# Inverse roots in ten instructions, and transposes moved by one product, in the z2 stage of a gated MLP

## The chip, the cores and the metric

One core of a Trainium2 chip runs the whole program. The time is the device time of one execution in microseconds (us). Engines are named as in the profile: PE is the matmul engine (PEld its weight loads), DVE the vector engine, ACT the scalar engine, POOL the GpSimd engine, SP the engine that only issues DMAs here.

## The reference

A block with two branches over 2048 rows of 576 features. The first branch normalises the rows, convolves them with a long kernel (a state-space model) and adds the result to x. The second branch is a gated MLP, and the change lies at its beginning:

```
h = _layernorm(x) * (1 + cb) + sb               # 2048 x 576
z = gelu(h @ w_in)                              # 2048 x 4608
z1 = z[:, :2304];  z2 = _layernorm(z[:, 2304:])
g = w_sp @ z2 + b_sp[:, None]                   # 2048 x 2048 by 2048 x 2304
x = x + gb * ((z1 * g) @ w_out)
```

The layer norm is `(x - mean) / sqrt(var + 1e-5)` over a row.

## The kernel before

The program runs three stages one behind the other. The first branch takes some 435 us. Then comes the z2 stage (`phase_a`), which computes z2 for all rows and stores it. The last stage (`phase_b`) computes z1, g and the output in four quarters.

In the z2 stage the rows are 16 tiles of 128, b = 0 to 15. All engines run the instructions in the order in which the Python code writes them: `self.tied` pins every instruction of an engine behind the one written before it, so the order of the calls is the order of each engine's queue. The loop `for b in range(1, 16)` writes one iteration per tile:

- `ln2_stats(b+3)`, `roots`, `ln2_rows(b+2)` (DVE): statistics, inverse root and normalised rows `n2` of a coming tile. In the profile the rows are written by two SCALAR_TENSOR_TENSOR and a COPY on `n`.
- `turn(b+1)` (PE): five transposes of `n2` with `ident` into the PSUM tile `pt`, of which there is one.
- `turn_hi(b+1)` (ACT) copies `pt` as fp16 into `nt`; `turn_lo(b+1)` (DVE) writes the rest, `pt - nt`, into the other half of `nt` and stores `nt` in DRAM (`n2_d`) on POOL's queue. A value is thus held as two fp16 numbers, and a product takes 14 matmuls per 512 columns. The first four need only the high part of `nt`, the ninth is the first to need the low part.
- `z2_mm(b, h)` (PE): five products `pz`, h = 0 to 3 of 512 columns and h = 4 of 256. `pz` has six PSUM buffers.
- `z2_gelu(b, h)` (ACT): gelu of a product into the two halves `z2` of the tile (1152 columns each; the profile calls them `z`). The pool has four such halves, so a tile's first gelu waits until the first half of the tile two before it has been stored.
- `z2_stats(b, c)` (DVE): statistics of six pieces of 384 columns (`bsz`). `roots(b-1, b+2)` takes the inverse roots of z2's variance of tile b-1 and of the coming tile's rows in one go (`rsqrt`, two columns `128x2`).
- `z2_diff(b-1)` (DVE, for even b-1 only) subtracts the halves; `z2_norm(b-1)` (ACT) applies the affine map with the root to both halves, `z<-z,nm,r` in the profile; `z2_store(b-1)` (POOL queue) stores them in `z2_d`.
- `do(b, LD)` to `do(b, V1)` are side work: weights of later stages are loaded, squared for their norms, scaled and split. In iterations 9 to 15 the side work prepares the blocks `wsp` of `w_sp`: `block_load` (SP) reads one into the single tile `xz`, `wsp_sums` (V0, DVE: three TENSOR_TENSOR on `xz`), `wsp_hi` (A1, ACT), `wsp_lo` (V1, DVE), and the next `block_load` waits for that `wsp_lo`.

`rsqrt` is also called four times in the first branch (`128x4`), and behind the loop `roots(15)`, `z2_norm(15)` and `z2_store(15)` end the stage. PE then has four products of z1 to do (`ps<-n2q,wf`), and needs from DVE and ACT the sets `zset` for g's first products (`ps<-wsp,zset`); the work on these stands behind `roots(15)` on DVE.

Of the kernel before, what the change touches and what calls it, by code (L numbers as in the profile page):

```python
# [9 lines left out]
F32 = mybir.dt.float32  # L10
F16 = mybir.dt.float16
BF = mybir.dt.bfloat16
I32 = mybir.dt.int32
AF = mybir.ActivationFunctionType
ALU = mybir.AluOpType
# [7 lines left out]
FH = 2304  # L23
# [166 lines left out]
def ssm(tc, I, x1_d, consts_s, dram, mod_d, mlp):  # L190
# [5 lines left out]
    with ExitStack() as ctx:  # L196
# [246 lines left out]
        def ln_stat(i, b):  # L443
# [22 lines left out]
            if b < 4:  # L466
                bs, mv = lnt[i]
                for h in range(2):
                    V.bn_stats(bs[:, b, h], x[:, b, HC * h:HC * h + HC])
                V.bn_aggr(mv[:, b], bs[:, b])  # L470
            else:
                mv = lnt.pop(i)[1]
                nm = ep.tile([128, 4], F32, name="nm")
                r = ep.tile([128, 4], F32, name="r")
                V.tensor_scalar(nm, mv[:, :, 0], -1.0, None, op0=ALU.mult)
                rsqrt(V, ep, r, mv[:, :, 1], 4)
                lns[i] = nm, r
# [497 lines left out]
def rsqrt(V, pool, r, var, n):  # L975

    vh = pool.tile([128, n], F32, name="vh%d" % n)
    q = pool.tile([128, n], F32, name="rq%d" % n)
    V.tensor_scalar(vh, var, 1e-5, 0.5, op0=ALU.add, op1=ALU.mult)
    V.tensor_single_scalar(q.bitcast(I32), vh.bitcast(I32), 1, op=ALU.logical_shift_right)  # L980
    V.tensor_scalar(r.bitcast(I32), q.bitcast(I32), -1, 0x5F3759DF - 0x400000, op0=ALU.mult, op1=ALU.add)

    for i in range(3):
        V.tensor_tensor(q, r, r, op=ALU.mult)
        V.tensor_tensor(q, q, vh, op=ALU.mult)
        if i < 2:
            V.scalar_tensor_tensor(r, q, 1.5, r, op0=ALU.subtract, op1=ALU.mult)
    V.tensor_scalar(q, q, -1.0, 1.5, op0=ALU.mult, op1=ALU.add)
    V.tensor_tensor(r, r, q, op=ALU.mult)


class Mixed:
# [7 lines left out]
class Mlp:  # L1000
# [428 lines left out]
    def z2_gelu(self, b, h):  # L1429
        n = min(512, FH - 512 * h)  # L1430
        if h == 0:
            self.zs[b] = [self.zp.tile([128, FH // 2], F32, name="z2", bufs=4) for _ in range(2)]
            self.bz[b] = self.ap.tile([128, 6, 6], F32, name="bsz")
        pm, c0 = self.pzs.pop((b, h)), 512 * h
        for i, z in enumerate(self.zs[b]):
            a, e = max(c0, FH // 2 * i), min(c0 + n, FH // 2 * (i + 1))
            if a < e:
                self.nc.scalar.activation(z[:, a - FH // 2 * i:e - FH // 2 * i], pm[:, a - c0:e - c0], AF.Gelu_apprx_tanh,
                                          scale=self.wcol(5 + h, INV_IN))
# [27 lines left out]
    def phase_a(self):  # L1467
        self.n2o, self.n2t, self.wrs = {}, {}, {}
        self.prods, self.z1s, self.n2, self.bsp, self.gbs, self.wfs = {}, {}, {}, {}, {}, {}
        ap = self.ap = self.pool(self.c2, "ap", 2)  # L1470
        cpa = ExitStack()
        self.pa = self.pool(cpa, "pa", 6, space=PSUM)
        self.ps1 = lambda: self.pa.tile([128, 512], F32, name="pz")
        self.zp = self.pool(self.c2, "zp", 2)
        self.wp = self.pool(self.ctx, "wp", 7, side="right")

        self.bq = self.pool(self.ctx, "bq", 1, side="right")
        self.cfp = self.ctx.enter_context(ExitStack())
        self.fp = self.pool(self.cfp, "fp", 1, side="right")
        self.wso = ap.tile([128, 4, 10, 128], F16, name="wso", bufs=1)  # L1480
        self.nc, plain = self.tied, self.nc
        self.nc.vector.memset(self.wso[64:, :, 9], 0.0)

        LD, PE, A0, A1, V0, V1 = range(6)
        sides = [[[] for _ in range(6)] for _ in range(17)]

        def side(b, k, fn, *a):
            sides[b][k].append((fn, a))

        def do(b, k):  # L1490
            for fn, a in sides[b][k]:
                fn(*a)

        for q in range(5):
            side(2 * q, LD, self.side_load, q)
            side(2 * q + 1, A0, self.side_sum, q)
            side(2 * q + 1, PE, self.win_scale, q)
            side(2 * q + 1, A1, self.side_hi, q)
            side(2 * q + 1, V1, self.side_last, q)
            side(2 * q + 1, V1, self.side_lo, q, 0)  # L1500
            side(2 * q + 2, V0, self.side_lo, q, 1)
        for h in range(2):
            side(1, LD, self.bsp_load, ap, h)
            side(2, A0, self.norm_bsp, h)
        for i in range(8):
            side(2 + i // 2, A1, self.wsp_load, 0, i, ap)
            side(3 + i // 2, A0, self.norm_sp, 0, i)
        for i in range(12):
            side(6 + i // 2, A1, self.out_load, ap, i)
            side(7 + i // 2, A0, self.norm_out, i)  # L1510
        for i in range(6):
            side(12 + i // 2, A1, self.wsp_load, 1, i, ap)
            side(13 + i // 2, A0, self.norm_sp, 1, i)
        side(13, V1, self.sums_out)
        side(14, PE, self.scales_out)
        side(6, V1, self.sums_sp, 0)
        side(7, PE, self.scales_sp, 0)
        side(11, PE, self.scales_gate, 0)
        side(12, PE, self.scale_p, 0)
        for i in range(7):  # L1520
            side(9 + i, V0, self.wsp_sums, i)
            side(9 + i, A1, self.wsp_hi, 0, i)
            side(9 + i, V1, self.wsp_lo, 0, i)
            side(8 + i, V1, self.block_load, 0, i)
        side(12, LD, self.z1_rows, 0)
        side(14, LD, self.bias_load, 0)
        for f, b in ((0, 14), (9, 15), (1, 15)):
            side(b, LD, self.z1_load, 0, f)


        self.turn(0)
        self.turn_hi(0)
        self.start_lo(2)
        self.start_load(4)
        self.x1_load(4)
        self.turn_lo(0)
        roots12 = self.ln2_two(1)
        do(0, LD)
        self.z2_mm(0, 0)
        do(0, A0)  # L1540
        self.start_sum(3)
        self.win_scale(8)
        self.z2_gelu(0, 0)
        self.start_hi(3)
        roots12()
        self.ln2_rows(1)
        do(0, PE)
        self.z2_mm(0, 1)
        self.z2_gelu(0, 1)
        self.start_sum(4)  # L1550
        self.z2_mm(0, 2)
        self.turn(1)
        self.start_lo(3)
        self.win_scale(9)
        self.turn_hi(1)
        self.start_hi(4)
        self.turn_lo(1)
        do(0, V0)
        self.z2_gelu(0, 2)
        self.z2_mm(0, 3)  # L1560
        do(0, A1)
        self.start_lo(4)
        self.ln2_rows(2)
        self.z2_stats(0, 0, 1, 2, 3)
        self.z2_gelu(0, 3)
        self.ln2_stats(3)
        do(0, V1)
        self.z2_stats(0, 4)
        self.z2_mm(0, 4)
        self.z2_gelu(0, 4)  # L1570
        for b in range(1, 16):
            do(b, LD)
            self.z2_mm(b, 0)
            do(b, A0)
            self.z2_gelu(b, 0)
            self.z2_stats(b - 1, 5)
            self.roots(b - 1, b + 2 if b + 2 < 16 else None)
            if b % 2:
                self.z2_diff(b - 1)
            self.z2_norm(b - 1)  # L1580
            if b + 2 < 16:
                self.ln2_rows(b + 2)
            if b + 4 < 16:
                self.x1_load(b + 4)
            self.z2_mm(b, 1)
            if b + 1 < 16:
                self.turn(b + 1)
            do(b, PE)
            self.z2_gelu(b, 1)
            self.z2_store(b - 1)  # L1590
            do(b, V0)
            self.z2_stats(b, 0, 1)
            if b + 1 < 16:
                self.turn_hi(b + 1)
            if b + 1 < 16:
                self.turn_lo(b + 1)
            self.z2_mm(b, 2)
            self.z2_gelu(b, 2)
            do(b, A1)
            self.z2_mm(b, 3)  # L1600
            self.z2_stats(b, 2, 3)
            self.z2_gelu(b, 3)
            if b + 3 < 16:
                self.ln2_stats(b + 3)
            do(b, V1)
            self.z2_stats(b, 4)
            self.z2_mm(b, 4)
            self.z2_gelu(b, 4)
        cpa.close()
        self.z2_stats(15, 5)  # L1610
        self.roots(15)
        self.z2_norm(15)
        self.z2_store(15)
        self.nc = plain
        self.c2.close()
# [652 lines left out]
S_H, I_H, S_O, I_O, N_S, N_O, N_H, N_B, _, T0, T1, HB, N_P = range(13)  # L2268
# [64 lines left out]
```

## Time and profile before

| | |
|---|---|
| median of 3 runs | 1771.88 us (1767.71, 1771.88, 1774.77) |
| profiled execution | 1768.14 us, of which its span of instructions is 1766.4 us; mean granted PE clock 0.988 |
| PE busy in the span | 1696.1 us (96%) |
| DVE, ACT, POOL busy | 1244.9 us (70%), 819.5 us (46%), 265.3 us (15%) |
| z2 stage on PE | first product at 437.9 us, last one ended at 676.4 us |

Read it so: over the whole program PE is nearly full, and the shares of the other engines are averages over three very different stages, so that the z2 stage has to be looked at by itself. A row of the timeline gives start, duration, engine, line, operation, tiles, and in brackets the idle time before it with what ended that. L154 is the helper through which all pinned instructions go, so the tiles tell them apart.

### The profile page before, as it was taken

To read this page: it belongs to the slowest core of one execution; us is meant where nothing else is said; L and a number is where in the kernel's file an instruction comes from. 1 tells how busy PE (TensorE), PEld (TensorE's weight loads), DVE (VectorE), ACT (ScalarE), POOL (GpSimd) and SP (SyncE) were. 2 spreads that over 40 slices of the span, in tenths; PEclk is the share of its full clock that TensorE was granted. 3 is DMA by queue.
4 is the path that set the end of the run, shared out by engine and by line. 5 is a ranking of instruction groups with operands and counts; after the bars stand their busy time and mean duration, and the time that the engine had idled before them with its cause. 6 is when DMAs were issued, how large, how long until landed. Compare 5 with 4: busy or idle time off the path is not lost.

```text
span 1766.4 us, 37058 instructions
## 1 busy us (share of the span) xinstructions
PE 1696.1 (96%) x15528; PEld 1256.4 (71%) x15528; DVE 1244.9 (70%) x2242; ACT 819.5 (46%) x1095; POOL 265.3 (15%) x413
## 2 busy tenths in 40 slices
PE   6889999997999999999999999999999999999999
PEld 2455555565455445778878888888888888888887
DVE  5984898857999997888898677788334477334432
ACT  3688799834577665455433443333232223122210
POOL 2252442242122111000000000000111100111100
PEclk9999999997999999999999999999999999999999
DMA  8466745789598889677665877774767563566531
GB/s 245 141 205 208 198 135 159 194 224 298 184 285 272 242 247 285 235 267 270 214 207 181 308 272 250 237 248 136 249 218 229 198 223 98 199 204 214 188 112 41
DMA packets 181741, 376.29 MB, mean 213 GB/s; under 512 B 38597, under 2 KB 101701, under 8 KB 180806
## 3 DMA queue, kind: packets, MB, share of 16 engines
q1 hardware_dynamic: 137782, 171.43, 32.3%
q0 software_dynamic: 37888, 175.83, 30.2%
q10 hardware_dynamic: 5904, 26.67, 3.7%
q8 instruction: 122, 2.00, 0.5%
q14 instruction: 45, 0.37, 0.1%
HBM read 263.12 MB, written 101.31 MB: 206 GB/s over the span
## 4 chain that ended last, share of the span: by engine, by line
PE 50%; DVE 19%; issue 5%; DMA 5%; ACT 2%; SPq 0%; POOL 0%; ACTq 0%; DVEq 0%; POOLq 0%
PE ps L154 47%; DMA zset<-set_d 3%; DVE bsz L154 2%; DVE zset L154 2%; DVE n L154 1%; DVE wsp L154 1%; DVE rq L154 1%; DVE raw L154 1%; DVE gt L154 1%; DVE z L154 1%; DVE wso L154 1%; DVE nt L154 1%; DVE rx L154 1%; DVE bsx L154 1%; PE pk L720 1%
## 5 line engine op out<-in xcount | busy, mean ns | idle before, releaser
L154 PEld LDWEIGHTS <-zset 128*128 128x128 f16 x7182 | 702.6, 98 | 94.9 <-DVE zset L154 7.3
L154 PE MATMUL ps<-wsp,zset 128*128 128x256 f16 x6048 | 669.2, 273 | 8.2 <-DVE zset L154 5.5
L154 PE MATMUL pz<-wz,nt 128*128 128x512 f16 (+1 forms) x1120 | 223.6, 359 | 8.4 <-ACT nt L154 3.1
L154 ACT ACTIVATE z<-gt 128x1024 f16<-128x1024 f32 x56 | 59.1, 1055 | 288.8 <-DVE gt L154 288.8
L154 PEld LDWEIGHTS <-nt 128*128 128x128 f16 x1120 | 109.5, 99 | 116.4 <-issue 5.3
L2041 POOL DMA_DIRECT2D zset<-set_d x96 | 51.1, 532 | 871.5 <-PE ps L154 622.8
L154 DVE SCALAR_TENSOR_TENSOR gt<-ps,sc,bsp 128x512 f32<-128x512 f32 x36 | 27.0, 750 | 206.4 <-PE ps L154 204.7
L154 PE MATMUL ps<-wout,z 128*128 128x288 f16 x1344 | 170.0, 286 | 0.0
L154 PEld LDWEIGHTS <-z 128*128 128x128 f16 x1344 | 131.5, 98 | 33.0
L154 PE MATMUL ps<-n2o,zset 128*128 128x256 f16 x1134 | 128.2, 273 | 0.0
L154 DVE TENSOR_TENSOR raw<-raw 128x512 f32<-128x512 f32 (+2 forms) x228 | 119.2, 529 | 12.3 <-DMA raw<-z_d 7.9
L154 DVE SCALAR_TENSOR_TENSOR gt<-ps,sc,gt 128x512 f32<-128x512 f32 (+1 forms) x180 | 122.3, 696 | 7.6
L154 ACT ACTIVATE zset<-raw 128x1792 f16<-128x1792 f32 x48 | 81.1, 1691 | 58.8 <-PE ps L154 23.8
L154 DVE TENSOR_TENSOR zset<-raw,zset 128x1792 f16<-128x1792 f32 x48 | 96.9, 2020 | 16.1 <-ACT zset L154 16.1
L154 DVE TENSOR_TENSOR z<-ps,z 128x512 f32<-128x512 f32 (+1 forms) x126 | 72.0, 599 | 37.2 <-ACT z L154 25.1
L154 ACT ACTIVATE wsp<-raw,sc 128x1792 f16<-128x1792 f32 x25 | 44.7, 1786 | 42.7 <-DVE raw L154 35.0
L154 ACT ACTIVATE z<-z,sc 128x1024 f32<-128x1024 f32 x21 | 24.1, 1149 | 76.0 <-DVE z L154 72.3
L154 ACT ACTIVATE z<-pz,sc 128x512 f32<-128x512 f32 (+1 forms) x96 | 51.7, 583 | 16.4 <-DMA z_d<-z 9.4
L154 ACT ACTIVATE z<-z,nm,r 128x1152 f32<-128x1152 f32 x24 | 31.5, 1343 | 52.9 <-DVE nm L154 29.8
L154 PE MATMUL ps<-n2q,wf 128*128 128x512 f16 x252 | 55.7, 379 | 0.0
L154 POOL DMA_DIRECT2D z_d<-z x32 | 32.4, 1014 | 135.2 <-ACT z L154 134.2
L154 PE MATMUL ps<-wout,z1b 128*128 128x288 f16 x384 | 52.4, 286 | 0.0
(354 smaller groups left out, 2501.4 us busy)
## 6 DMA issues: line engine op xcount, KB each, us to landing
zset<-set_d POOLq DMA_DIRECT2D x96, 896.0 KB, 5.0
raw<-z_d SPq DMA_DIRECT2D x48, 512.0 KB, 5.8
set_d<-zset ACTq DMA_DIRECT2D x24, 896.0 KB, 6.8
z_d<-z POOLq DMA_DIRECT2D x32, 576.0 KB, 9.7
zset<-wa_d POOLq DMA_DIRECT2D x18, 896.0 KB, 5.0
raw<-in_w_spT SPq DMA_DIRECT2D x25, 512.0 KB, 6.2
set_d<-zset SPq DMA_DIRECT2D x12, 896.0 KB
u_d<-st1o POOLq DMA_DIRECT2D x32, 288.0 KB, 3.2
```

The costliest lines, as they stand in the source:

```text
L154: return self.tc.keep_in_program_order(f(*a, **k))
L720: T.matmul(pm[:, w * j:w * j + w], cst[k // 8][:, k % 8], k1t[c][:, k, :w], start=True, stop=True)
L2041: self.nc.gpsimd.dma_start(o, self.set_d[f, j - 1] if j else self.wa_d[f])
```

## The change

1. `rsqrt` uses 10 instructions in place of 13: two steps, the second of higher order, in place of three Newton steps. All callers are affected, 22 calls in all.
2. In the loop, `turn(b+1)` moves from behind `z2_mm(b, 1)` to behind `z2_mm(b, 0)`; `turn_hi(b+1)` moves on ACT from behind `z2_gelu(b, 1)` to behind `z2_gelu(b, 0)`, ahead of `z2_norm(b-1)`; `turn_lo(b+1)` moves on DVE from behind `z2_stats(b, 0, 1)` to a place ahead of `ln2_rows(b+2)`, and its store ahead of `z2_store(b-1)` on POOL's queue.
3. The pool of z2's halves has five buffers in place of four.

```
-    V.tensor_scalar(vh, var, 1e-5, 0.5, op0=ALU.add, op1=ALU.mult)
+    V.tensor_scalar(vh, var, 1e-5, 0.5 / 2.25, op0=ALU.add, op1=ALU.mult)
     V.tensor_single_scalar(q.bitcast(I32), vh.bitcast(I32), 1, op=ALU.logical_shift_right)
-    V.tensor_scalar(r.bitcast(I32), q.bitcast(I32), -1, 0x5F3759DF - 0x400000, op0=ALU.mult, op1=ALU.add)
-
-    for i in range(3):
-        V.tensor_tensor(q, r, r, op=ALU.mult)
-        V.tensor_tensor(q, q, vh, op=ALU.mult)
-        if i < 2:
-            V.scalar_tensor_tensor(r, q, 1.5, r, op0=ALU.subtract, op1=ALU.mult)
-    V.tensor_scalar(q, q, -1.0, 1.5, op0=ALU.mult, op1=ALU.add)
-    V.tensor_tensor(r, r, q, op=ALU.mult)
+    V.tensor_scalar(r.bitcast(I32), q.bitcast(I32), -1, 0x5F3759DF - 0x400000 - 0x80000000, op0=ALU.mult, op1=ALU.add)
+    V.tensor_tensor(q, r, r, op=ALU.mult)
+    V.tensor_tensor(q, q, vh, op=ALU.mult)
+    V.scalar_tensor_tensor(r, q, 1.5, r, op0=ALU.subtract, op1=ALU.mult)
+    V.tensor_tensor(q, r, r, op=ALU.mult)
+    V.tensor_tensor(q, q, vh, op=ALU.mult)
+    V.scalar_tensor_tensor(vh, q, -5.0 / 3, q, op0=ALU.add, op1=ALU.mult)
+    V.scalar_tensor_tensor(r, vh, 1.25, r, op0=ALU.add, op1=ALU.mult)
...
-            self.zs[b] = [self.zp.tile([128, FH // 2], F32, name="z2", bufs=4) for _ in range(2)]
+            self.zs[b] = [self.zp.tile([128, FH // 2], F32, name="z2", bufs=5) for _ in range(2)]
...
             self.z2_mm(b, 0)
             do(b, A0)
+            if b + 1 < 16:
+                self.turn(b + 1)
             self.z2_gelu(b, 0)
+            if b + 1 < 16:
+                self.turn_hi(b + 1)
             self.z2_stats(b - 1, 5)
             self.roots(b - 1, b + 2 if b + 2 < 16 else None)
             if b % 2:
                 self.z2_diff(b - 1)
             self.z2_norm(b - 1)
+            if b + 1 < 16:
+                self.turn_lo(b + 1)
             if b + 2 < 16:
                 self.ln2_rows(b + 2)
             if b + 4 < 16:
                 self.x1_load(b + 4)
             self.z2_mm(b, 1)
-            if b + 1 < 16:
-                self.turn(b + 1)
             do(b, PE)
             self.z2_gelu(b, 1)
             self.z2_store(b - 1)
             do(b, V0)
             self.z2_stats(b, 0, 1)
-            if b + 1 < 16:
-                self.turn_hi(b + 1)
-            if b + 1 < 16:
-                self.turn_lo(b + 1)
             self.z2_mm(b, 2)
```

How the queues stand in iteration b = 12. On ACT before, the copies of `pt` into `nt` stand behind the two halves of the affine map (`z<-z,nm,r`), which wait for DVE's root, and behind the second product's gelu:

```order
L154 ACTIVATE z_7331<-pz,sc 128x512
L154 ACTIVATE z_7160<-z_7160,nm_7354,r_7353 128x1152
L154 ACTIVATE z_7161<-z_7161,nm_7354,r_7353 128x1152
L154 ACTIVATE z_7331<-pz,sc 128x512
L154 ACTIVATE nt<-pt 128x512
L154 ACTIVATE nt<-pt 128x128
```

On ACT now, in the same iteration:

```order
L154 ACTIVATE z_7286<-pz,sc 128x512
L154 ACTIVATE nt<-pt 128x512
L154 ACTIVATE nt<-pt 128x128
L154 ACTIVATE z_7118<-z_7118,nm_7309,r_7308 128x1152
L154 ACTIVATE z_7119<-z_7119,nm_7309,r_7308 128x1152
L154 ACTIVATE z_7286<-pz,sc 128x512
```

The two copies have passed the two halves of the affine map and a gelu.

On DVE before, the end of the root (`rq`, `rx`), the affine map's operands (`r`, `nm`) and the coming rows `n`; and, some rows further in the same iteration, the sums of a block of w_sp (`xz`), two statistics and then the low part of `nt`:

```order
L154 TENSOR_TENSOR rq_7339<-rq_7339,vh_7338 128x2
L154 TENSOR_SCALAR rq_7339<-rq_7339 128x2
L154 TENSOR_TENSOR rx<-rx,rq_7339 128x2
L154 TENSOR_SCALAR r_7353<-rx 128x1
L154 SCALAR_TENSOR_TENSOR nm_7354<-mvx,r_7353 128x1
L154 SCALAR_TENSOR_TENSOR n_7359<-x1t,mvx,mrow 128x576
L154 SCALAR_TENSOR_TENSOR n_7359<-n_7359,rx,mrow 128x576
L154 COPY n_7359<-n_7359 128x64
```

Further on, on DVE before:

```order
L154 TENSOR_TENSOR xz<-xz 128x512
L154 TENSOR_TENSOR xz<-xz 128x256 x2
L154 BN_STATS bsz<-z_7331 128x6 x2
L154 TENSOR_TENSOR nt<-pt,nt 128x512
L154 TENSOR_TENSOR nt<-pt,nt 64x128
L154 BN_STATS bsz<-z_7331 128x6
```

On DVE now:

```order
L154 TENSOR_TENSOR rq_7297<-rq_7297,vh_7296 128x2
L154 SCALAR_TENSOR_TENSOR vh_7296<-rq_7297 128x2
L154 SCALAR_TENSOR_TENSOR rx<-vh_7296,rx 128x2
L154 TENSOR_SCALAR r_7308<-rx 128x1
L154 SCALAR_TENSOR_TENSOR nm_7309<-mvx,r_7308 128x1
L154 TENSOR_TENSOR nt<-pt,nt 128x512
L154 TENSOR_TENSOR nt<-pt,nt 64x128
L154 SCALAR_TENSOR_TENSOR n_7317<-x1t,mvx,mrow 128x576
L154 SCALAR_TENSOR_TENSOR n_7317<-n_7317,rx,mrow 128x576
L154 COPY n_7317<-n_7317 128x64
```

The low part of `nt` has passed the rows `n`, the scale factors that some iterations compute there, the sums on `xz` and two statistics. On POOL's queue the store `n_d<-nt` of iteration 12 stood behind the two stores `z_d<-z` of tile 11 and now stands ahead of them.

## The prediction

> **What bounds the kernel now.** I looked first at the busy time by stretches of the z2 stage, then at PE's timeline there, then at who waits on DVE, and last at DVE's own timeline. The stretches, with the columns start:end, length, busy us and instructions of PE, PEld, DVE, ACT, POOL, granted PE clock, DMA share and GB/s:
>
> ```profile
> 464.00:592.00 128.00, 128.00 (x686) 67.50 (x685) 117.79 (x371) 93.57 (x153) 33.24 (x45) 1.00 0.85 260
> 592.00:655.00 63.00, 58.03 (x306) 29.73 (x305) 59.00 (x168) 38.96 (x60) 10.55 (x13) 1.00 0.78 227
> 655.00:677.00 22.00, 22.00 (x120) 11.47 (x118) 18.08 (x58) 15.49 (x22) 4.61 (x5) 1.00 0.96 288
> ```
>
> To 592 us PE is full; from 592 to 655 it isn't. DVE is as good as full in both: its idle 10.2 us over 371 instructions and 4.0 us over 168 are 27 and 24 ns an instruction, the gap from one to the next and no wait. Who waits on DVE from 464 to 690 us (total, times, longest) confirms it:
>
> ```profile
> DVE xz L154 <- DMA xz<-in_w_spT: 1.6, 1, 1.6
> DVE bsz L154 <- ACT z L154: 1.1, 1, 1.1
> ```
>
> So there are two bounds, PE up to 592 us and DVE nearly everywhere. PE's timeline shows where the one holds up the other. The transposes `pt` of the next tile come once a tile:
>
> ```profile
> 563.59 0.71 PE L154 MATMUL pt<-ident,n 128*128 128x128 f32 x5
> 564.13 13.78 PE L154 MATMUL pz<-wz,nt 128*128 128x512 f16 x70
> 577.75 0.71 PE L154 MATMUL pt<-ident,n 128*128 128x128 f32 x5
> ...
> 592.05 0.71 PE L154 MATMUL pt<-ident,n 128*128 128x128 f32 x5
> ...
> 607.38 0.71 PE L154 MATMUL pt<-ident,n 128*128 128x128 f32 x5
> ...
> 619.74 4.49 PE L154 MATMUL pz<-wz,nt 128*128 128x512 f16 x20 [1.71 <-DVE nt L154]
> 624.06 0.71 PE L154 MATMUL pt<-ident,n 128*128 128x128 f32 x5
> ...
> 639.25 0.71 PE L154 MATMUL pt<-ident,n 128*128 128x128 f32 x5
> ...
> 654.53 0.71 PE L154 MATMUL pt<-ident,n 128*128 128x128 f32 x5
> ```
>
> A tile that waits for nothing takes 577.75 - 563.59 = 14.16 us. From 592.05 to 654.53 four tiles take 62.48 us, 5.84 more than 4 x 14.16. They wait for `nt`, the transposed rows of the next tile. The periods are 15.33, 16.68, 15.19 and 15.28 us, so against a PE that never waited, `nt` is late by 1.17, 3.69, 4.72 and 5.84 us for tiles 11 to 14.
>
> **The change, part by part: `nt` earlier.** These are DVE's rows of iteration 11:
>
> ```profile
> 608.83 0.16 DVE L154 TENSOR_TENSOR rq<-rx 128x2 f32<-128x2 f32 x1
> 609.03 0.16 DVE L154 TENSOR_TENSOR rq<-rq,vh 128x2 f32<-128x2 f32 x1
> ...
> 612.34 0.81 DVE L154 SCALAR_TENSOR_TENSOR n<-x1t,mvx,mrow 128x576 f32<-128x576 f32 x1
> ...
> 614.15 0.21 DVE L154 TENSOR_SCALAR sc<-sc 128x1 f32<-128x1 f32 x1
> ...
> 616.42 1.61 DVE L154 TENSOR_TENSOR xz<-xz 128x512 f32<-128x512 f32 x3
> 617.94 1.01 DVE L154 BATCH_NORM_STATS2 bsz<-z 128x6 f32<-128x384 f32 x2
> 618.99 1.02 DVE L154 TENSOR_TENSOR nt<-pt,nt 128x512 f16<-128x512 f32 x2
> ```
>
> From start to start the rows `n` take 614.15 - 612.34 = 1.81 us, the sums on `xz` 1.52, two statistics 1.05. The low part of `nt` moves ahead of all these, 4.38 us, and in iterations with scale factors ahead of those too (2.27 here). One instruction of the root costs 609.03 - 608.83 = 0.20 us from start to start, each waiting for the one before, also in the new form: three fewer are 0.59 us a root. By iterations 10, 11, 12 and 13 the low part is thus earlier by at least 4.38 + 0.59 k, k = 1 to 4, which is 4.97, 5.56, 6.14 and 6.73 us, each above its lateness (1.17, 3.69, 4.72, 5.84). On ACT the high part passes the affine map, which waits for the root, so it no longer hangs on DVE at all. All 5.84 us go. The moved instructions cost nothing in themselves: five transposes, two copies, two subtractions and one store as before.
>
> What is late next: DVE writes the rows `n` now behind the low part, which takes 1.05 us, and PE wants them one product earlier. A product of 512 columns is (577.75 - 564.13)/4.5 = 3.03 us. The tightest place is iteration 14, for tile 15. PE without waits would have stood at the old place at 592.05 + 4 x 14.16 = 648.69, at the new one at 645.66. The rows were done, before, at:
>
> ```profile
> 646.39 0.20 DVE L154 COPY n<-n 128x64 f32<-128x64 f32 x1
> ```
>
> That is 646.59; less four roots (2.35) and plus 1.05 it is 645.29. The margin is 0.4 us, and what DVE has gained before tile 10 comes on top. I take no wait.
>
> **DVE's end.** DVE is full, so its savings add up to the end of the stage unless its feed stops it. In iteration 9 the low part stands right behind the subtraction of z2's halves, and wants the high part from ACT:
>
> ```profile
> 569.72 0.67 ACT L154 ACTIVATE z<-pz,sc 128x512 f32<-128x512 f32 x1
> 570.29 0.74 ACT L154 ACTIVATE nt<-pt 128x512 f16<-128x512 f32 x2
> 570.93 1.78 ACT L154 ACTIVATE z<-pz,sc 128x128 f32<-128x128 f32 x4
> ...
> 575.63 0.19 ACT L154 ACTIVATION_READ_ACCUMULATOR wsst<-wsst 128x1 f32 x1
> 578.52 0.69 ACT L154 ACTIVATE z<-pz,sc 128x512 f32<-128x512 f32 x1 [2.70 <-PE pt L154]
> ...
> 578.47 1.36 DVE L154 TENSOR_TENSOR z<-z,z 128x1152 f32<-128x1152 f32 x1
> ```
>
> ACT is free at 575.82, but tile 9's first gelu starts only at 578.52. The page puts that down to PE's transposes, but the product it reads ended one product ahead of 577.75, at 574.72, so I read it as the wait for a store that frees z2's buffer. The fifth buffer takes that wait away: the first half of tile 9 then needs a store of tile 6, not of 7. The gelu takes 570.29 - 569.72 = 0.57 us and the two copies 0.64, so the high part is there at 577.03. DVE's subtraction ended, from 578.47 on, about 1.28 later, at 579.75. So up to tile 9 DVE can gain no more than 2.7 us on its feed, though ten roots would give 5.9. PE's own start of the stage moves too: tile 0 waits for DVE there, behind a root.
>
> ```profile
> 449.17 0.74 PE L154 MATMUL pt<-ident,n 128*128 128x128 f32 x5 [0.26 <-DVE n L154]
> ...
> 456.55 7.29 PE L154 MATMUL pz<-wz,nt 128*128 128x256 f16 x38 [0.96 <-DVE wz L154]
> ```
>
> The last wait is longer than 0.59 us, so that root's 0.59 moves PE and DVE alike. That makes 3.3 us for DVE at tile 9 and 0.59 + 5.84 = 6.43 for PE's end of the stage. Behind tile 9 come seven more roots. The one of iteration 15 gains nothing, as the end shows:
>
> ```profile
> 672.79 1.61 DVE L154 TENSOR_TENSOR xz<-xz 128x512 f32<-128x512 f32 x3 [1.57 <-DMA xz<-in_w_spT]
> ...
> 682.92 0.16 DVE L154 SCALAR_TENSOR_TENSOR nm<-mvx,r 128x1 f32<-128x1 f32 x1
> ...
> 676.40 12.25 PE L154 MATMUL ps<-n2q,wf 128*128 128x512 f16 x56
> ...
> 689.47 4.76 PE L154 MATMUL ps<-wsp,zset 128*128 128x256 f16 x42 [0.60 <-DVE zset L154]
> 695.52 4.65 PE L154 MATMUL ps<-wsp,zset 128*128 128x256 f16 x41 [1.30 <-DVE zset L154]
> ```
>
> DVE waits 1.57 us there for the load of the last block, which starts when iteration 14 ends; a shorter root only lengthens that wait. Six roots remain, 3.5 us, and DVE's last root ends 3.3 + 3.5 = 6.8 us earlier, at 683.08 - 6.8 = 676.3.
>
> **The sum.** From 695.52 on PE has work without a gap for a long time, so its start there carries the time. It stands 12.4 us behind DVE's last root, and 19.12 us behind PE's end of the stage, 1.90 of which are the two waits. Afterwards: by DVE 676.3 + 12.4 = 688.7, by PE 676.40 - 6.43 + 17.2 = 687.2. The later one decides: 6.8 us earlier than 695.52. The profiled execution took 1768.14 us and would take 1761.3. It lies 3.7 us below the median of the three runs, 1771.88, so for a median I forecast 1765.1.
>
> Bounds of what the profile doesn't show. DVE's gain to tile 9 lies between 0 and 5.9 us; I take the feed's 3.3, since every saving reaches it and the feed is read from rows. The load of the last block may come later than now, as the DMA engines are at 0.96 in that stretch; a DVE gain of 3.5 is the low end. The roots of the first branch may move PE where it waits behind them:
>
> ```profile
> PE pk L154 <- DMA uu<-v_d: 6.3, 4, 3.5
> PE pk L154 <- DVE et L154: 1.3, 1, 1.3
> PE pk L154 <- DVE kab L154: 0.9, 3, 0.6
> ```
>
> Two of those, 0.59 each, make 1.2 at most; I take 0, because that branch ends in waits for the DMAs of `v_d`. On POOL's queue the store of `nt` passes the two stores of z2, which wait for ACT's affine map. The low part of `nt` ends 1.05 us behind the root, or 2.33 where the subtraction stands between, the map's first half about 1.3 behind it; with the issue of one more store ahead (1.0 us, an estimate), z2's stores start 1 to 2 us later. With five buffers ACT has the time, as the third rival works out.
>
> [...]
>
> **The rivals.** First, DVE keeps nothing of the savings before tile 9, or the last block's load comes that much later: 3.5 us, 1768.4. For it speaks the DMA share of 0.96, against it that the load's start moves with DVE. Second, more goes: PE's 6.43, its two waits of 1.90 at the end, and 1.2 in the first branch, 9.5 us in all, 1762.4. It needs a DVE that outruns the feed worked out above. Third, slower: z2's stores. How long stores and loads of z2's halves take to land, minimum, median and longest, and ACT's two affine maps, the second group's 2.59 us for both halves:
>
> ```profile
> DMA to landing us min/median/max: 5.6/9.7/13.0
> 657.45 2.59 ACT L154 ACTIVATE z<-z,nm,r 128x1152 f32<-128x1152 f32 x2 [2.86 <-DVE nm L154]
> ```
>
> The store of a tile's first half must have landed before ACT's gelu of the third product of two tiles on, which writes the half that reuses its buffer. I count from the first product of the iteration that stores it, in iteration 11. That product began two products ahead of 607.38, at 601.32, or at 600.15 without PE's 1.17. The root ended ahead of the subtraction and the rows, at 612.34 - 1.28 = 611.06, 10.9 us on; less DVE's 3.3 it is 7.6. With both maps, and 1.0 us as my estimate for the other store's issue, it is 11.2, landed at the median 20.9. The gelu comes a tile, the transposes and three products on, 14.16 + 0.54 + 3 x 3.03 = 23.8. The margin is 2.9 us, so this mechanism decides from a landing of 12.6 us on. If all landed in 14.6 us, ACT and then DVE would lose 2 us in each of six tiles, 12 us, and the kernel would come out 5.2 us slower, 1777.1. Against it: the median is 9.7, and four buffers demanded more.
>
> **How the numbers follow.** The forecast (a gain of 5 to 8 us) gets 0.66, the first rival 0.15, the second 0.13, the third 0.06. 0.5% is 8.9 us, about what runs that spread over 7.1 us can tell from no change. Only the second rival exceeds it by itself; with the spread of a median of three, a little of the forecast does too: faster 0.2, same 0.75, slower 0.05. The range takes in the first two rivals, 1762.4 to 1768.4, and half the runs' spread, 3.5 us, on each side: 1758.9 to 1771.9.
>
> **What would show it.** Right: PE's busy time in the four tiles from 592 us on has no wait for `nt`, transposes 14.16 us apart throughout; DVE waits up to 1 us for `nt` from ACT in tiles before 10; the waits of ACT's gelu for z2's stores vanish; DVE's last root ends near 676 us; PE's second run of `ps<-wsp,zset` starts near 688.7 and still waits one to two us before. Wrong: PE waiting at the transposes for `n`, ACT waiting at a third product for a store of z2, or DVE waiting longer for `xz` would each say which step failed.

## The result: slower by 1.2%, and the profile after

The changed kernel took 1792.22 us (median of four executions, 1783.55 to 1795.31) against 1770.61 before (four executions too): a ratio of 1.0121, with an interval of 1.01 to 1.0143. I had forecast 1765.1. The profile below is of the execution of 1783.55 us, whose span is 1781.6 us. It is the least slow of the four, so the other three lost more than these views show.

The same three stretches of the z2 stage as shown of before, and three of 10 us inside the first one:

```profile
464.00:592.00 128.00, 120.35 (x624) 62.44 (x623) 101.19 (x309) 81.00 (x131) 29.51 (x40) 0.97 0.75 226
592.00:655.00 63.00, 60.84 (x317) 30.77 (x315) 57.10 (x158) 41.46 (x65) 11.44 (x14) 1.00 0.81 248
655.00:677.00 22.00, 20.43 (x112) 10.62 (x110) 20.04 (x61) 15.67 (x24) 5.18 (x6) 1.00 0.88 235
530.00:540.00 10.00, 7.67 (x36) 3.75 (x35) 5.92 (x18) 8.58 (x16) 2.56 (x3) 0.83 0.37 112
540.00:550.00 10.00, 9.48 (x51) 4.80 (x49) 7.25 (x25) 2.51 (x5) 1.14 (x2) 1.00 1.02 288
550.00:560.00 10.00, 6.93 (x27) 3.17 (x28) 6.66 (x14) 9.20 (x14) 3.68 (x5) 0.83 0.59 197
```

In the first stretch PE was full before (128.00 of 128.00); now it isn't, and DVE has fallen from 117.79 to 101.19 us busy. The loss is where I had seen no problem. In the 10 us from 530 even the DMA engines are mostly idle (0.37), and in the next 10 us they are full (1.02) while ACT is busy for only 2.51 us. So the engines wait for one another in turn, and the waits from 464 to 690 us say for whom (total, times, longest):

```profile
ACT wsst L154 <- DMA wsst<-in_w_spT: 23.9, 7, 8.3
DVE nt L154 <- ACT nt L154: 21.1, 4, 8.6
ACT wsst L154 <- DMA wsst<-in_w_out: 17.5, 7, 5.5
PE pz L154 <- ACT nt L154: 6.4, 3, 3.6
```

ACT thus waits 41.4 us for the loads of `wsst`. Before, it waited 5.6 us for them in all, and DVE for ACT's `nt` not at all. `wsst` is side work that the prediction never named: SP loads two pieces of later weights in every iteration (`wsp_load` and `out_load`, slot A1), and ACT squares them for their norms in the next iteration (slot A0, ahead of z2's first gelu). PE's timeline shows what it costs there:

```profile
517.74 0.71 PE L154 MATMUL pt<-ident,n 128*128 128x128 f32 x5
...
533.50 4.83 PE L154 MATMUL pz<-wz,nt 128*128 128x512 f16 x14 [2.33 <-ACT nt L154]
538.17 0.71 PE L154 MATMUL pt<-ident,n 128*128 128x128 f32 x5
...
553.07 4.88 PE L154 MATMUL pz<-wz,nt 128*128 128x512 f16 x14 [3.59 <-ACT nt L154]
557.79 0.71 PE L154 MATMUL pt<-ident,n 128*128 128x128 f32 x5
```

The tiles are 20.43 and 19.62 us apart, not 14.16. And the product after each wait takes 4.7 us from its start to the transposes, not 3.03. One round of what holds it up, by the timelines of ACT, DVE and SP of the changed kernel:

```profile
531.24 1.06 ACT L154 ACTIVATE wsst<-wsst 128x1024 f32<-128x1024 f32 x1 [0.73 <-DMA wsst<-in_w_spT]
...
532.86 0.75 ACT L154 ACTIVATE nt<-pt 128x512 f16<-128x512 f32 x2
...
533.64 1.02 DVE L154 TENSOR_TENSOR nt<-pt,nt 128x512 f16<-128x512 f32 x2 [8.63 <-ACT nt L154]
534.69 0.82 DVE L154 SCALAR_TENSOR_TENSOR n<-x1t,mvx,mrow 128x576 f32<-128x576 f32 x1
...
535.54 0.34 SPq L154 DMA_DIRECT2D x1t<-x_d  x1
535.97 0.95 SPq L154 DMA_DIRECT2D wsst<-in_w_spT  x2
...
550.80 1.06 ACT L154 ACTIVATE wsst<-wsst 128x1024 f32<-128x1024 f32 x1 [8.29 <-DMA wsst<-in_w_spT]
```

Read it as a ring. ACT squares the second piece at 531.24; the gelu and the copies `nt` stand behind it. DVE's low part had waited 8.63 us for these copies. The rows `n` now stand behind the low part. SP's load of `x1t` waits for the first of these rows, and the next loads of `wsst` stand behind it on SP's queue. They land, and ACT squares at 550.80. The round takes 19.56 us: about 5.2 from the square to the issue of the second load, 14.3 for its landing (landing is the time from the issue of a load to the arrival of its data). While these two come to more than PE's 14.16, each tile is late by the difference. In this profile that holds for two tiles, which cost PE 6.27 and 5.46 us; behind 557.79 the transposes are 14.16 to 16.17 us apart. Landing is the long part, as the chain of waits shows too:

```profile
515.78 15.37 DMA wsst<-in_w_spT
...
536.46 14.26 DMA wsst<-in_w_spT
```

The kernel before had nearly as long a landing once, without the ring. These are the loads on SP's queue there, and the square of the second one:

```profile
510.53 1.01 SPq L154 DMA_DIRECT2D wsst<-in_w_spT  x2
522.79 0.34 SPq L154 DMA_DIRECT2D x1t<-x_d  x1
```

```profile
522.36 1.06 ACT L154 ACTIVATE wsst<-wsst 128x1024 f32<-128x1024 f32 x1 [3.77 <-DMA wsst<-in_w_spT]
```

Some 11 us passed from the issue to the square. But DVE wrote the rows right behind the root, whether ACT's copies were there or not, and SP went on at 522.79, when the square had only just begun. Nothing went round. Why a landing takes 14 to 15 us in the changed kernel and some 11 in this place before isn't taken apart here; that the DMA engines were full from 540 to 550 us fits other traffic, but no run shows which.

The end of the stage adds to it. SP's and DVE's last steps in the changed kernel, with the landing by the chain of waits, and PE's start of what follows:

```profile
680.09 0.37 SPq L154 DMA_DIRECT2D xz<-in_w_spT  x1
...
683.78 2.10 SPq L154 DMA_DIRECT2D raw<-z_d  x3
683.78 18.55 DMA raw<-z_d
...
697.84 0.16 DVE L154 SCALAR_TENSOR_TENSOR nm<-mvx,r 128x1 f32<-128x1 f32 x1
702.45 1.15 DVE L154 TENSOR_TENSOR raw<-raw 128x256 f32<-128x256 f32 x2 [4.45 <-DMA raw<-z_d]
...
705.44 0.61 PE L154 MATMUL ps<-wsp,zset 128*128 128x256 f16 x2 [5.73 <-ACT zset L154]
```

DVE's last root ends at 698.00, not at 683.08. The loads `raw`, which the next stage begins with, stand on SP's queue behind the load of `xz`, which waits for DVE. They go out 14.33 us later than before (683.78 against 669.45), no more than DVE's own 14.92, but the first takes 18.55 us to land. So DVE waits 4.45 us for it. Before, it didn't wait at all:

```profile
683.09 2.67 DVE L154 TENSOR_TENSOR raw<-raw 128x256 f32<-128x256 f32 x5
```

There the load had landed within 13.6 us. Why it takes longer with the change isn't shown either.

A measure that all runs share is used below: the **stage** counts from PE's first product of z2 to its 45th matmul `ps<-wsp,zset` (the row at 695.52 of before). It leaves out the first branch, whose length alone moves by up to 14 us between these profiles, and what follows the stage, which takes 1070.8 us in the profile of before and 1067.3 to 1070.5 in the others. The stage took 257.6 us before and 275.1 with the change. Each stage below is that of one profile; the two of the changed kernel differ by 0.3 us.

### The profile page after: what moved, and what is told of

Same layout as the page of the kernel before. It is cut to its first block, busy times and chain, and to the rows that moved or that the text cites. A ratio compares the mean times of both kernels' runs of the same rounds, so it can differ in the third digit from the quotient of the medians.

```text
span 1781.6 us, 36998 instructions
## 1 busy us (share of the span) xinstructions
PE 1702.1 (96%) x15528; PEld 1257.5 (71%) x15528; DVE 1235.9 (69%) x2176; ACT 820.5 (46%) x1095; POOL 264.3 (15%) x413
## 4 chain that ended last, share of the span: by engine, by line
PE 55%; DVE 12%; DMA 8%; issue 4%; ACT 2%; SPq 0%; POOL 0%; ACTq 0%; DVEq 0%; POOLq 0%
PE ps L154 52%; DMA wsst<-in_w_spT 3%; DMA zset<-set_d 2%; DMA wsst<-in_w_out 2%; DVE zset L154 1%; DVE gt L154 1%; DVE bsz L154 1%; DMA raw<-z_d 1%; DVE n L154 1%; ACT z L154 1%; DVE wsp L154 1%; DVE raw L154 1%; PE pk L720 1%; DVE nt L154 0%; DMA uu<-v_d 0%
## 5 line engine op out<-in xcount | busy, mean ns | idle before, releaser
L154 DVE SCALAR_TENSOR_TENSOR wsp<-raw,sc,wsp 128x1792 f16<-128x1792 f32 x25 | 51.9, 2078 | 0.0
L154 DVE TENSOR_TENSOR gt<-gt,z 128x1024 f32<-128x1024 f32 x28 | 34.3, 1225 | 22.3 <-ACT z L154 21.6
```

What stands on the lines that cost most here:

```text
L154: return self.tc.keep_in_program_order(f(*a, **k))
```

## The experiments

Each edit is against the changed kernel unless said otherwise. Theory A is the ring. The kernel before ran again with each group of kernels, hence the several medians in its row; each ratio is to the runs of before in its group.

| kernel | stage us | median us | ratio to before, interval |
|---|---|---|---|
| before | 257.6 | 1768.28 to 1770.61 | 1 |
| changed | 275.1 | 1792.22 | 1.0121, 1.01 to 1.0143 |
| changed, again | 274.8 | 1785.36 | 1.0103, 1.0083 to 1.0122 |
| rows_first | 253.3 | 1761.03 | 0.9956, 0.9934 to 0.9977 |
| x1_behind | 254.4 | 1762.56 | 0.9957, 0.994 to 0.9975 |
| hi_first | 252.4 | 1765.50 | 0.9986, 0.9968 to 1.0003 |
| both_cut | 254.7 | 1763.58 | 0.9973, 0.9949 to 0.9997 |
| half_loads | 256.1 | 1766.70 | 0.9996, 0.9976 to 1.0015 |
| after_b4 | 270.8 | 1790.83 | 1.0134, 1.0112 to 1.0156 |
| roots_only | 252.9 | 1761.38 | 0.996, 0.9937 to 0.9983 |
| old_roots | 276.8 | 1785.82 | 1.0092, 1.0058 to 1.0125 |
| roots_bufs | 252.1 | 1762.67 | 0.9974, 0.9957 to 0.999 |
| rows_first_old | 259.7 | 1769.06 | 0.9998, 0.9982 to 1.0013 |
| rows_first_sums | 254.7 | 1762.17 | 0.9973, 0.9955 to 0.999 |

**The ring cut on DVE (rows_first).**

```
             self.z2_norm(b - 1)
-            if b + 1 < 16:
-                self.turn_lo(b + 1)
             if b + 2 < 16:
                 self.ln2_rows(b + 2)
             if b + 4 < 16:
                 self.x1_load(b + 4)
+            if b + 1 < 16:
+                self.turn_lo(b + 1)
```

> The changed kernel with one step moved: DVE writes the rows n of tile b+2 (and SP issues the load of x1t that waits for them) ahead of the low part of nt, not behind it. Theory A (a ring): ACT's squares on wsst wait for SP's loads of wsst, the copies of nt wait behind these squares, DVE's low part of nt waits for the copies, the rows n wait behind the low part, the load of x1t on SP waits for the rows, and the next loads of wsst stand behind it. Ring: 14 to 15 us from issue to the squares plus some 5 us, about 20 us a tile against 14.16. Moved like this, the load of x1t no longer hangs on nt, so the waits of DVE for nt (21.1 us in all) and of ACT for wsst (41.4 us) shrink to under 8 and 15, PE keeps its period, and the time is 1761 to 1770 us. Rival B (traffic alone): the loads of wsst land late because z2's stores now go out half a microsecond ahead of them; then the landings stay at 12 to 15 us, ACT still waits for wsst in the tiles before 590 us, and the time stays above 1778.

The waits that were 41.4 and 21.1 us, from 460 to 720 us, are these, and PE's transposes are 14.16 to 14.52 us apart again:

```profile
ACT wsst L154 <- DMA wsst<-in_w_spT: 7.2, 3, 4.8
DVE nt L154 <- ACT nt L154: 1.6, 1, 1.6
```

```profile
528.64 0.71 PE L154 MATMUL pt<-ident,n 128*128 128x128 f32 x5
542.80 0.71 PE L154 MATMUL pt<-ident,n 128*128 128x128 f32 x5
557.32 0.71 PE L154 MATMUL pt<-ident,n 128*128 128x128 f32 x5
```

One step moved turns a loss of 1.2% into a gain of 0.44%. A landing of nearly 12 us comes here too, once, and passes without an echo: ACT's square waits, SP's next loads don't.

```profile
505.14 0.97 SPq L154 DMA_DIRECT2D wsst<-in_w_spT  x2
517.33 0.34 SPq L154 DMA_DIRECT2D x1t<-x_d  x1
...
517.59 1.06 ACT L154 ACTIVATE wsst<-wsst 128x1024 f32<-128x1024 f32 x1 [2.25 <-DMA wsst<-in_w_spT]
```

**The ring cut on SP (x1_behind).**

```
-            if b + 4 < 16:
-                self.x1_load(b + 4)
             ...
             do(b, A1)
+            if b + 4 < 16:
+                self.x1_load(b + 4)
```

> The changed kernel with only SP's queue reordered in the loop: the load of x1t for tile b+4 stands behind the loads of wsst of its iteration instead of ahead of them. The engines' orders stay. Theory A (ring through SP's queue): the loads of wsst no longer wait for the rows n, only for their buffer (ACT's squares of the iteration), so they go out some 3 to 5 us earlier and the ring is cut; the time is 1761 to 1770 us. Rival B (traffic alone): as slow as the changed kernel, above 1778, since the same bytes go out beside z2's stores. Rival C: the load of x1t is late in its place and DVE waits for it: a wait of DVE for x1t appears.

No engine's order changes, only SP's, and the time is 0.43% below before. ACT waits for `wsst` nowhere from 460 to 720 us, and DVE never for `x1t`, so rival C falls; so does rival B, with the same bytes going out. The loads go out when ACT's squares have freed their buffers:

```profile
520.44 0.19 ACT L154 ACTIVATION_READ_ACCUMULATOR wsst<-wsst 128x1 f32 x1
...
520.66 1.41 SPq L154 DMA_DIRECT2D wsst<-in_w_spT  x2
524.82 0.34 SPq L154 DMA_DIRECT2D x1t<-x_d  x1
```

**The roots and the order apart (roots_only, old_roots).** The kernel before with the new `rsqrt`, and the changed kernel with the old one.

> The kernel before with the ten-step roots alone; order and buffers as before. Theory A: without the moved copies there is no ring; DVE keeps the savings, its last root ends 5 to 6 us earlier than 683.08 and the time falls by 4 to 6 us, 1765 to 1768. Rival D (the faster root itself disturbs the stage: DVE ahead of its feed, stores and loads collide): no gain or slower, 1771 or more, with ACT waits for wsst over 15 us in all.

> The changed kernel with the thirteen-step root of before: the moved transposes, copies and low part and the five buffers alone. Theory A: the ring is in the order, so this is as slow as the changed kernel or slower by up to 6 us: 1784 to 1800, with DVE waiting over 15 us for nt and ACT over 30 us for wsst. Rival D (the shorter roots are what upsets the stage): no slower than before, 1766 to 1773.

The roots alone bring 0.4% (interval 0.17 to 0.63%). The stage and DVE's last root came 4.8 us earlier, a little less than the 5 to 6 expected; the median fell by 7.2, more than expected, but by its interval anything from 3 to 11 us. The order with five buffers alone costs 0.92%, and its waits are the ring's:

```profile
ACT wsst L154 <- DMA wsst<-in_w_spT: 20.9, 5, 7.7
DVE nt L154 <- ACT nt L154: 17.4, 4, 5.8
ACT wsst L154 <- DMA wsst<-in_w_out: 12.2, 7, 4.9
```

Rival D falls: the shorter roots upset nothing.

**The ring cut on ACT (hi_first).**

```
             self.z2_mm(b, 0)
-            do(b, A0)
             ...
                 self.turn_hi(b + 1)
+            do(b, A0)
```

> The changed kernel with ACT's squares on wsst moved behind z2's first gelu and the two copies of nt (they stood ahead of them). Everything else stays: the low part ahead of the rows n, the load of x1t ahead of the loads of wsst. Theory A (the ring): this cuts its third link, the copies no longer wait for the loads of wsst, so the low part, the rows and the next loads go out in time; from z2's first product to PE's second run of ps<-wsp,zset it takes 252 to 256 us (changed kernel 275.1, before 257.6) and the time is 1759 to 1768 us. Rival B (the loads of wsst themselves are too slow for ACT): ACT still waits over 30 us for wsst and, since its affine maps and gelus stand behind the squares, the time stays above 1778.

The stage is as forecast, and the wait of 41.4 us is down to these two:

```profile
ACT wsst L154 <- DMA wsst<-in_w_spT: 0.9, 1, 0.9
ACT wsst L154 <- DMA wsst<-in_w_out: 0.8, 1, 0.8
```

So the third link is one too. The time is 0.14% below before, and its interval includes no change. That it gained less than the other cuts isn't shown, since the intervals overlap; the one profile (1761.69 us) is of one of the faster executions (1760.24 to 1771.48), so it can't say what the slower ones lost.

**Both cuts (both_cut)**: the edits of rows_first and hi_first together.

> The changed kernel with the ring cut at two places: the rows n and the load of x1t ahead of the low part, and ACT's squares behind the copies of nt. If one cut already removes all that the ring costs, this is like either alone: stage 251.5 to 253.5 us, 1758 to 1764.

The time is inside the forecast, the stage 1.2 us above it. A second cut brings nothing.

**Half the bytes (half_loads).** The loads and squares of `wsst` take half of the columns; the order is that of the change.

```
-        t = self.wss[i] = self.norm_tile(pool)[:, :864]
+        t = self.wss[i] = self.norm_tile(pool)[:, :432]
...
+            t = self.wss[i] = self.norm_tile(pool)[:, :512].rearrange("p (k n) -> p k n", k=2)
```

> The changed kernel with its order untouched, but every load of wsst brings half of its columns and ACT's squares read that half: half of the sum of squares over w_sp (of these blocks) and w_out is left out. It shortens the ring by what the landing and the two squares lose. Theory A: from 14 to 15 us to the squares it falls under 10, and the ring (landing plus 4 to 5 us) under 14.16, so the stage takes 252 to 257 us and the time is 1759 to 1768. Rival (what counts is the low part ahead of the rows n on DVE, or z2's stores, not the loads): still above 265 us and 1778.

The stage fell from 275.1 to 256.1, inside the forecast. The ring isn't gone but short, with waits of a third to a half (440 to 720 us):

```profile
ACT wsst L154 <- DMA wsst<-in_w_spT: 10.9, 4, 3.8
DVE nt L154 <- ACT nt L154: 8.0, 4, 3.9
```

Where ACT waits for two tiles running, its squares of the second piece start at 523.09 and 537.34, a round of 14.25 us in place of 19.56, about PE's 14.16. From 440 to 700 us the loads of `wsst` from `in_w_spT` landed in 6.1 us at the median, against 13.0 with the change. The landing is thus the size that decides, with the order of all queues left alone. ACT's squares read half as much too, but with the change each took no more than 1.06 us, a small part beside the 6.9 us of landing.

**Four buffers (after_b4).**

> The changed kernel with four buffers for z2's halves as before. Theory A: the ring doesn't run through these buffers, so the stage takes 270 to 282 us, as with five. Rival: the fifth buffer lets z2's stores pile up with the loads, and with four it is under 262.

```profile
DVE nt L154 <- ACT nt L154: 21.4, 6, 7.2
ACT z L154 <- DMA z_d<-z: 13.9, 6, 3.1
```

As slow as with five (two executions). ACT's waits for z2's stores are back, and no cost of theirs shows beside the ring. **The buffers with the roots (roots_bufs)** take the waits away where there is no ring:

> The kernel before with the ten-step roots and the five buffers for z2's halves, its order as before. Theory A: the fifth buffer only removes ACT's waits for z2's stores (5.6 us in all with the roots alone), which DVE's supply feels before tile 9; stage 251 to 253 us, 0 to 2 us under the roots alone (252.9), time 1759 to 1764. Rival: the waits move on to the squares or the copies and it stays at 253, 1761 to 1764, no difference.

0.8 us of stage, and no difference of time that can be told from the roots alone.

**The moved copies by themselves (rows_first_old)**: rows_first with the old `rsqrt`.

> The order without the ring (transposes and copies early, the rows n and the load of x1t ahead of the low part) and five buffers, with the thirteen-step roots of before. What the move of nt is worth by itself. The prediction put all of PE's 5.84 us of waits for nt down as won, but DVE, full to the end, sets the start of what follows. If DVE bounds, the stage takes 256 to 258 us against 257.6 before and the time is that of before, 1766 to 1771; if PE's waits count, 252 to 254 us and 1762 to 1765.

259.7 us, 1.7 above the forecast, and a ratio of 0.9998: the early copies take PE's waits for the high part away and are worth nothing, since DVE sets the end: PE finishes z2 3.0 us earlier than before, counted from its first product, and DVE's last root comes 0.7 us later. With the short roots it is the same. rows_first and roots_bufs differ only in the moved instructions, with stages of 253.3 and 252.1 us and ratios of 0.9956 and 0.9974, whose intervals overlap. So what rows_first gains on the kernel before is, as far as these runs can tell, the roots' gain.

**The last loads (rows_first_sums)**: rows_first with `z2_stats(b, 0, 1)` ahead of `do(b, V0)` for b = 14 and 15.

> The order without the ring and the ten-step roots, with DVE's two statistics ahead of the sums on xz in the last two tiles, where DVE waits 4.9 us for the load of xz. If these waits set DVE's end, about 1 us of work fills each of them: stage 251.3 to 252.5 us against 253.3, time 1 to 2 us lower, 1759 to 1760; if ACT's map on xz or the later load takes it back, 253 to 254 and no change.

The stage missed both forecasts: 254.7 us, 1.4 above rows_first. DVE's wait for `xz` is gone from the list, but DVE now waits 7.8 us for ACT's gelus and 1.9 us for ACT's part of `wsp`.

**The change again (after_again).**

> The changed kernel itself, once more, for the spread of its time. Theory A (the ring keeps itself going as long as a tile's landing and the 5 us behind it come to more than 14.16 us): the stage again takes 270 us or more, with DVE waiting over 15 us for nt, and executions differ by how many tiles the ring holds on for, 1780 to 1797. If the first profile caught a chance state, the stage would now take under 262 us.

```profile
DVE nt L154 <- ACT nt L154: 23.1, 6, 9.0
ACT wsst L154 <- DMA wsst<-in_w_spT: 21.9, 5, 8.2
ACT wsst L154 <- DMA wsst<-in_w_out: 17.8, 8, 5.1
```

The ring is no accident of one execution.

## Why the prediction was wrong

- **The step that failed** is "The moved instructions cost nothing in themselves", with its price for the new order on DVE, "DVE writes the rows `n` now behind the low part, which takes 1.05 us". The rows took over the low part's wait for ACT as well, up to 8.63 us; and SP's loads, which stand behind a load that waits for these rows, went out late with them. That closed the ring. Moving the low part back behind the rows and that load, and nothing else, takes the loss away (rows_first: 275.1 to 253.3 us of stage).
- **What hid it** is "it no longer hangs on DVE at all", said of the high part on ACT. It no longer waits for the root, but its copies stand behind the squares, as they did before, and the squares wait for SP's loads, which hang on DVE's rows through the load of `x1t`. I had quoted a row of these squares (575.63, `wsst`) and read it as ACT's being free, without asking what sets its end. And I named POOL's queue and not SP's: nobody moved an SP instruction, but the one that SP waits for moved.
- **DVE "waits up to 1 us for `nt`"**: 21.1 us, in four waits.
- **The root's price** held for the instruction: in the changed kernel too its rows take 0.16 us and start 0.20 us apart (546.16, 546.36, 546.55). Of the sum, less came. The roots alone shorten DVE's part, from z2's first product to its last root's end, by 4.8 us (245.2 to 240.4). The forecast's 6.8 for the whole change was too large even without the ring: rows_first has 240.9, 4.3 less than before, and roots_bufs 239.6, 5.6 less. In rows_first DVE waits 4.9 us for `xz`, not 1.57, so the last block's load "comes that much later", the first rival's second half.
- **"All 5.84 us go"**: with the ring cut PE's period is 14.16 us again to the end. That DVE's end, the later one, and not PE's carries the time held as well (rows_first_old).
- **The rival for slower** named the wrong queue. No wait of ACT for z2's stores is left in the list of the changed kernel, and four buffers were as slow as five. The 1.0 us estimated for the issue of a store is what a store of z2's took on POOL's queue before (1.01 us at 568.87, `z_d<-z`); the store of `nt`, the one that moved, took 0.54 us (573.04).

## What to carry to other kernels

When an instruction moves ahead in a queue, everything behind it takes over its waits (here the rows `n` those of the low part, up to 8.63 us): follow each to a DMA queue's next issue, and from there back to the engine that reads the load. If the path closes, add up one round and compare it with the period of the loop; a landing of some 11 us cost PE nothing before (510.53 to 522.36, PE busy for 128.00 of 128.00 us from 464 on), while one of 14.26 us in a ring cost it all by which the round exceeded the period (19.56 against 14.16 us, the tile late by 5.46 us). A queue in which no instruction moved (SP here) is part of the change when what it waits for has moved.

## What the runs showed of the hardware

A wait of PE cost more than its length here. After the waits of 2.33 and 3.59 us the matmuls of 512 columns started 0.43 us apart instead of 0.215, from 533.50 to 536.88 and from 553.95 to 557.35; the granted clock is 0.50 in both, and 0.83 in the two of 10 us from 530 and from 550. Each of these adds about 1.7 us. In old_roots, behind a wait of 2.74 us (619.88), six such matmuls took 2.44 us and the five transposes behind them 1.27, where elsewhere in that profile they took 1.47 (667.44) and 0.71 us (560.34); in the changed kernel's other profile, whose longest wait of PE for `nt` was 5.1 us, the granted clock was 0.56 from 555 to 560 us. A wait of 1.73 us in the changed kernel was not followed by such half speed (granted clock 1.00 from 523.20 to 526 us), nor one of 1.51 us in old_roots (667.44, six matmuls in 1.47 us). From which wait on the clock falls, what else has a part in it, and what sets the 3.4 us of the first two stretches isn't shown.
